# Storing output chunks as sixteen runs of rows, and loading the value block in 64 + 8 partitions

## The chip, the cores and the metric

The kernel runs on one core of one Trainium2 chip. The metric is the device time of one execution in microseconds (us), the median of repeated runs; lower is better. A separate execution is recorded by the hardware profiler, and all views below are of that one.

## What is computed

Two operators in a row. First an attention whose keys and values are averaged over groups of eight tokens; then a mixture of experts with one chosen expert per token, in which the chosen expert's answer is weighted by its probability.

```python
# q, k, v: (8 batches, 8 heads, 576 tokens, 64), float32
k_p = k.reshape(B, H, 72, 8, D).mean(axis=3)          # 72 groups of 8 tokens
v_p = v.reshape(B, H, 72, 8, D).mean(axis=3)
attn = softmax(q @ k_p.T / sqrt(D))
x = (attn @ v_p), heads side by side                  # (4608 tokens, 512)
logits = unit(x) @ unit(expert_emb).T / tau           # 8 experts
e = argmax(logits);  gate = softmax(logits)[e]
out = gate * (relu(x @ w1[e]) @ w2[e])                # w1 512x1024, w2 1024x512
```

The output is 4608 rows of 512 float32, 576 rows per batch.

## The kernel before, in words

**One batch after the other, 576 tokens each.** With T = 36, a token of a batch is `i * 36 + t`: i is one of 16 runs of 36 consecutive tokens, t the place in the run. `flat` (L295) puts (head, run) on the 128 partitions for q and k. `grouped` (L298) puts the 72 groups on partitions for v, so the value tile `vv` has 72 partitions. Loads are issued by GpSimd, which casts float32 to fp16 on the way.

**The steps of a batch** are made in `attention` (from L386) and `ffn` (from L732):

- `load_v` (L889) loads v in one transfer. For batch 0 `mean_raw` (L602) and `v_sum` (L455), both on TensorE, make the mean and the group sums from it; for later batches VectorE adds (L445, L449). From the mean of v, `guess` (L615) and `guess_end` choose one expert for the whole batch. GpSimd reads that choice into a register and issues the loads of the expert's w1 and w2 (`load_w1` L319, `load_w2` L324), or skips them where one of four held pairs of weights is that expert's already.
- The 36 places in a run are cut in three units of 12, u = 0, 1, 2: `score` (L471), `exp` (L478), `pv` (L489), `x_scale` (L499, L501), and `x_turn` (L507), a VectorE transpose in blocks of 32 that brings 192 tokens of x into `xt_all`, features on partitions. Columns of `xt_all` are ordered by place and then by run (`t * 16 + i`).
- `square` (L516) and `route` (L530) give the router's logits; `route_out`, `root` (GpSimd), `prob` and `gate` make the gate per token.
- `h_part` (L749) is the first layer: eight slices `w` of 128 hidden features, four matmuls of each block of tokens. The first two slices (`early` = 2) are done in three blocks of 192 tokens, so that they can start once the first unit is turned; the others in two blocks of 288. `relu` (L758) moves the sums to `hT`.
- `y_part` (L769) is the second layer, by chunks of 128 tokens (c = 0 to 3), and `y_last` (L798) the last 64 tokens. `y_out` (L786, L788) scales by the gate, and `store` (L877) writes the chunk to the output, through SyncE's queue, in the last batch through ScalarE's queue too.

**What a store looks like.** A chunk's 128 partitions are 8 places times 16 runs, place first. `out_rows` (L864) describes the destination in that order: 8 places outermost, 16 runs inside, rows of 2 KB. The last 64 tokens are two stores of 4 places by 16 runs by 1 KB.

**What orders the work.** Every step is entered in a `Plan` with an engine, a cost, what it waits for, a priority, PSUM tiles (`NPS` = 4) and, for loads and stores, a cost on the DMA rings. `order` places steps greedily, `improve` tries 400 random changes of the priorities and keeps what lowers the planned end of TensorE's work over six random draws. The steps are then emitted in that order on each engine; each engine works through its own list strictly. So a changed cost or dependence can change the order of the whole kernel. Where the plan has TensorE idle, `warm` (L371) emits filler matmuls on a tile of ones: one for 0.22 us of planned idle time, with slower ones reckoned in the first 5.5 us; from planned time 28 on only where over 0.4 us are idle, and for 65% of that.

**The end.** A loop (L1068) handles batches in which some token chose another expert than the batch's guess. It has as many rounds as a number made on the chip, and in this data none. On entering it, every engine waits for the transfers still in flight. After the loop the last full chunk, kept in `y_end`, is stored in two halves of 64 partitions, one from SyncE (L1113) and one from ScalarE (L1114).

Of the kernel before, what the change touches and what calls it, by code (L numbers as in the profile page):

```python
# [242 lines left out]
def kernel(  # L243
# [54 lines left out]
    def grouped(a, b):  # L298
        return a[b].rearrange("h (g r) d -> g h (r d)", r=POOL)
# [56 lines left out]
    def cols(c):  # L356
        return ds(c * 128, min(128, S - c * 128))


    def warm(slot, idle, t):  # L360

# [24 lines left out]
    def attention(b, early=False):  # L386
# [117 lines left out]

        def x_turn(u):

            nc.vector.transpose(  # L507
                out=xt_all[:, b].rearrange("p w (t l) -> p t w l", l=32)[:, ts(u, 6)],
                in_=st['x', u].rearrange("p b j d -> p (b j d)").rearrange(
                    "p (t l w) -> p t w l", w=4, l=32))  # L510

        def square(u):
            if 'sq' not in st:
                st['sq'] = xp.tile([128, 4, S], BF16, name="sq", bufs=1)
            cs = ts(u, 192)
            nc.scalar.activation(out=st['sq'][:, :, cs], in_=xt_all[:, b, :, cs],  # L516
                                 func=AF.Square)

# [185 lines left out]
        for u in range(NU):  # L704
            step(f's{u}', 'PE', 0.53, lambda u=u: score(u),
                 ['kT', f'q{u}', (f'pv{u}', b - 1)], b - 10, tiles=2)
            for p in range(2):
                step(f'e{u}{p}', 'ACT', 0.71, lambda u=u, p=p: exp(u, p), [f's{u}'], b - 5,
                     frees=[(f's{u}', p)])
            step(f'pv{u}', 'PE', 0.55, lambda u=u: pv(u), ['v', f'e{u}0', f'e{u}1'],  # L710
                 b - 10, tiles=1)
            step(f'xs{u}', 'DVE', 1.18, lambda u=u: x_scale(u), [f'pv{u}'], b - 1.5,
                 frees=[(f'pv{u}', 0)])
            step(f'x{u}', 'DVE', 0.92, lambda u=u: x_turn(u), [f'xs{u}'], b - 1.6)
            step(f'sq{u}', 'ACT', 0.75, lambda u=u: square(u),
                 [f'x{u}', ('route', b - 1)], b - 4)

        step('route', 'PE', 0.86, route,
             ['sq0', 'sq1', 'sq2', 'emb', ('h', 0, b), ('gate', b - 2)], b - 0.02, tiles=1)
# [12 lines left out]
    def ffn(plan, b, xt, w, get_gm, finish, last=False, early=0):  # L732
# [9 lines left out]
        def h_part(w, u):  # L742


            n, step_ = (SU, 256) if w < early else (HALF, 512)
            if u == 0:
                st['ph', w] = psum(plan)
            for kk in range(4):
                nc.tensor.matmul(out=st['ph', w][:, ds(u * step_, n)],  # L749
                                 lhsT=w1v[:, kk, w // 4, (w // 2) % 2, w % 2, :],  # L750
                                 rhs=xt()[:, kk, ts(u, n)],
                                 start=(kk == 0), stop=(kk == 3))

        def relu(w):
            n, step_ = (SU, 256) if w < early else (HALF, 512)
            if ('hT', w // 4) not in st:
                st['hT', w // 4] = hp_.tile([128, 2, 2, S], FP16, name=f"hT{w // 4}")
            nc.scalar.activation(  # L758
                out=st['hT', w // 4][:, (w // 2) % 2, w % 2, :].rearrange(
                    "p (r c) -> p r c", c=n),  # L760
                in_=st['ph', w].rearrange("p (r c) -> p r c", c=step_)[:, 0:S // n, 0:n],
                func=AF.Relu)

        def y_part(c, part):
            if part == 0 and (last or c % 2 == 0):
# [57 lines left out]
        for w, u in order:  # L823
            end = 2 if w < early else 1
            xs = before('lw1' if w < 4 else 'lw1b', 'copy',
                        *(f'x{i}' for i in range(u + 1 if w < early else u + 2)))
            hs[w, u] = chain(0.33 if w < early else 0.495, lambda w=w, u=u: h_part(w, u), xs,
                             tiles=int(u == 0))
# [12 lines left out]
        for part in parts:  # L841
            if part is None:
                o = chain(0.98, y_last, before('lw2', 'copy') + relus, 1)
                plan.step('ACT', 1.4 if last else 0.85, y_last_out, [o, *gm], -10 + pri,
                          frees=[(o, 0)], store=0.45)
                continue
            c, half = part
            ys[c, half] = chain(0.865, lambda c=c, half=half: y_part(c, half),
                                before('lw2', 'copy') + relus[4 * half:4 * half + 4],
                                tiles=int(half == 0 and (last or c % 2 == 0)))  # L850
            if half:
                o = ys[c if last else c // 2 * 2, 0]
                if last:
                    plan.step('DVE' if c % 2 == 0 else 'ACT', 0.7 if c % 2 == 0 else 1.2,
                              lambda c=c: y_out(c), [ys[c, 1], *gm], -10 + pri,
                              frees=[(o, 0)], store=0.82)
                elif c % 2:
                    for i in (c - 1, c):
                        plan.step('ACT', 0.6, lambda i=i: y_out(i), [ys[i, 1], *gm],
                                  -10 + pri, frees=[(o, 0)] if i == c else [], store=0.82)  # L860
        if b is not None:
            done['y', b] = prev[0][0]

    def out_rows(o_b, c, y_sb):  # L864

        rows = o_b.rearrange("(i t) d -> t i d", t=T)
        if c < 4:
            return [(rows[ts(c, 8)], y_sb)]
        DH = DM // 2
        return [(rows[32:T, :, ts(j, DH)], y_sb[ts(j, 64), 0:DH]) for j in range(2)]  # L870

    def store(b):
        o_b = out[ts(b, S)]
# [8 lines left out]
    with tc.manual_schedule():  # L882
# [6 lines left out]
        def load_v(b, after=()):  # L889
            def emit():  # L890
                vv = loads['v', b] = inp.tile([G, H, POOL * D], FP16, name="vv")
                nc.gpsimd.dma_start(out=vv, in_=grouped(v, b))
            done['lv', b] = load(0.9, 3.6, emit, [('v', b - 2), ('vs', b - 2), *after])

        def load_q(b, units=(NU,), u=0):
            def emit(cs):
# [213 lines left out]
            px.run()  # L1110

    for dst, src in out_rows(out[ts(B - 1, S)], 3, y_end):
        nc.sync.dma_start(out=dst[0:4], in_=src[0:64])  # L1113
        nc.scalar.dma_start(out=dst[4:8], in_=src[64:128])  # L1114

# [1 line left out]
_INS = ['q', 'k', 'v', 'moe_expert_emb', 'moe_tau', 'moe_w1', 'moe_w2']  # L1117
# [31 lines left out]
```

The softmax here doesn't subtract the row's maximum and nothing guards it: scores larger than these inputs give would overflow.

## Time and profile before

| | |
|---|---|
| time, median of 3 runs | 216.98 us (216.51 to 219.39) |
| the profiled execution | 220.48 us, span 218.8 us |
| mean granted TensorE clock | 0.941 |
| busy: TensorE / VectorE / ScalarE / GpSimd | 194.6 / 143.9 / 126.3 / 35.3 us |
| loads through GpSimd's queue | 24.65 MB, 61.8% of 16 DMA engines' span |
| stores through SyncE's queue | 9.00 MB, 12.8% of 16 DMA engines' span |

The span runs from the first to the last instruction of the profiled execution. A busy time is a sum over the span; it does not tell whether a stage waited. The granted clock is the share of full speed that TensorE was given; it is either 1 or 0.5 at a moment here. The share of a DMA queue is the time that its packets took, over 16 engines and the whole span.

### The profile page before, as it was taken

To read this page: it belongs to the slowest core of one execution; us is meant where nothing else is said; L and a number is where in the kernel's file an instruction comes from. 1 tells how busy PE (TensorE), PEld (TensorE's weight loads), DVE (VectorE), ACT (ScalarE), POOL (GpSimd) and SP (SyncE) were. 2 spreads that over 40 slices of the span, in tenths; PEclk is the share of its full clock that TensorE was granted. 3 is DMA by queue.
4 is the path that set the end of the run, shared out by engine and by line. 5 is a ranking of instruction groups with operands and counts; after the bars stand their busy time and mean duration, and the time that the engine had idled before them with its cause. 6 is when DMAs were issued, how large, how long until landed. Compare 5 with 4: busy or idle time off the path is not lost. (4 is left out here: it accounts for less than half of the span.)

```text
span 218.8 us, 7393 instructions
## 1 busy us (share of the span) xinstructions
PE 194.6 (89%) x3155; PEld 121.6 (56%) x3156; DVE 143.9 (66%) x391; ACT 126.3 (58%) x203; POOL 35.3 (16%) x61
## 2 busy tenths in 40 slices
PE   6869999998996999998898899989998999999910
PEld 2345477454873468555674487538753865486500
DVE  3644948559598943976699669775977894732200
ACT  3034526386476367557674967586758767775200
POOL 7107016000410007003010511041000020020000
PEclk9985589998898799999999999999999999999995
DMA  5997999999997148999994799999975500330131
GB/s 81 180 161 116 206 216 181 202 216 229 252 216 133 27 108 195 202 219 190 235 219 86 164 186 235 226 208 230 234 180 128 186 32 3 99 115 9 45 130 52
DMA packets 18486, 34.63 MB, mean 158 GB/s; under 512 B 2440, under 2 KB 9224, under 8 KB 17936
## 3 DMA queue, kind: packets, MB, share of 16 engines
q0 software_dynamic: 12992, 24.65, 61.8%
q1 hardware_dynamic: 5184, 9.00, 12.8%
q8 instruction: 26, 0.43, 0.8%
q10 hardware_dynamic: 272, 0.46, 0.6%
q14 instruction: 12, 0.10, 0.1%
HBM read 61.88 MB, written 9.44 MB: 326 GB/s over the span
## 5 line engine op out<-in xcount | busy, mean ns | idle before, releaser
L749 PE MATMUL pa<-xt_all,w 128*128 128x288 f16 (+1 forms) x576 | 68.7, 276 | 1.1 <-DVEq L666 0.6
L769 PE MATMUL pa<-w,hT 128*128 128x512 f16 x256 | 62.7, 386 | 4.0 <-ACT y_sb L786 2.8
L749 PEld LDWEIGHTS <-w 128*128 128x128 f16 x576 | 53.2, 99 | 14.5 <-issue 3.8
L758 ACT ACTIVATE hT<-pa 128x576 f16<-128x576 f32 x64 | 40.7, 647 | 19.2 <-PE pa L749 18.5
L478 ACT ACTIVATE at<-pa 72x768 f16<-72x768 f32 x48 | 36.6, 803 | 12.5 <-PE pa L471 12.1
L769 PEld LDWEIGHTS <-hT 128*128 128x128 f16 x256 | 23.4, 98 | 30.4 <-issue 6.6
L786 ACT ACTIVATE y_sb<-pa,gm 128x512 f32<-128x512 f32 x29 | 19.1, 685 | 25.0 <-PE pa L769 25.0
L516 ACT ACTIVATE sq<-xt_all 128x768 bf16<-128x768 f16 x24 | 20.0, 841 | 10.4 <-DVE xt_all L507 10.2
L432 DVE STREAM_TRANSPOSE qT<-qq 128x768 f16<-128x768 f16 x24 | 22.6, 961 | 3.9 <-DMA qq<-in_q_dram 3.6
L501 DVE TENSOR_TENSOR x_sb<-pa,rc 128x768 f16<-128x768 f32 x24 | 23.0, 957 | 0.8
L507 DVE STREAM_TRANSPOSE xt_all<-x_sb 128x768 f16<-128x768 f16 x24 | 22.9, 965 | 0.3
L371 PE MATMUL pa<-ones_m 128*128 128x512 f16 x58 | 18.7, 470 | 1.7 <-DVE half_c L975 1.7
L319 POOL DMA_DIRECT2D w<-in_moe_w_dram x10 | 4.2, 417 | 97.5 <-DMA w<-in_moe_w_dram 40.6
L499 DVE RECIPROCAL rc<-pa 128x12 f32<-128x12 f32 x24 | 5.3, 222 | 21.1 <-PE pa L489 20.6
L547 POOL TENSOR_TENSOR rn<-lgT,half_c 128x5 f32<-128x5 f32 x8 | 9.5, 1189 | 58.8 <-DVE lgT L552 58.8
L471 PE MATMUL pa<-qT,kT 32*72 32x192 f16 x384 | 14.6, 257 | 3.2 <-DVE kT L423 1.8
L489 PEld LDWEIGHTS <-at 72*32 72x32 f16 x1152 | 12.1, 101 | 8.9 <-ACT at L478 4.6
L489 PE MATMUL pa<-vpx,at 72*32 72x65 f16 x1152 | 15.0, 203 | 1.9 <-ACT at L478 1.4
L471 PEld LDWEIGHTS <-kT 32*72 32x72 f16 x384 | 8.6, 111 | 11.8 <-issue 5.6
L552 DVE STREAM_TRANSPOSE lgT<-pa 128x160 f32<-128x160 f32 x8 | 2.8, 349 | 16.4 <-PE pa L530 16.4
L445 DVE TENSOR_TENSOR vv<-vv 72x2048 f16<-72x2048 f16 (+1 forms) x14 | 13.1, 935 | 0.2
L371 PEld LDWEIGHTS <-ones_m 128*128 128x128 f16 x58 | 6.2, 115 | 9.0 <-issue 4.7
(98 smaller groups left out, 152.6 us busy)
## 6 DMA issues: line engine op xcount, KB each, us to landing
w<-in_moe_w_dram POOLq DMA_DIRECT2D x14, 1024.0 KB, 16.1
out_dram<-y_sb SPq DMA_DIRECT2D x30, 256.0 KB
kk<-in_k_dram POOLq DMA_DIRECT2D x8, 576.0 KB, 16.9
vv<-in_v_dram POOLq DMA_DIRECT2D x8, 576.0 KB, 25.0
qq<-in_q_dram POOLq DMA_DIRECT2D x7, 576.0 KB, 16.5
w<-in_moe_w_dram POOLq DMA_DIRECT2D x4, 512.0 KB, 6.3
out_dram<-y_sb SPq DMA_DIRECT2D x15, 64.0 KB
qq<-in_q_dram POOLq DMA_DIRECT2D x1, 384.0 KB
```

The source lines that it names most:

```text
L371: nc.tensor.matmul(out=pa[:, 0:512], lhsT=ones_m[:, 0:128], rhs=ones_m[:, 0:512], start=True, stop=True)
L432: nc.vector.transpose(out=qT.rearrange("p w r (t i) -> p t w r i", i=16), in_=qq.rearrange("p t (w r i) -> p t w r i", w=2, r=2))
L471: nc.tensor.matmul(out=pS[a // 2][0:G, ds(a % 2 * 512 + r * SU, SU)], lhsT=kT[ts(a, 32), w, r, :], rhs=qT[ts(a, 32), w, r, :], start=(w == ...
L478: nc.scalar.activation(out=at.rearrange("g a r c -> g a (r c)"), func=AF.Exp, scale=escale, in_=st['pS', u][p][0:G].rearrange("g (a c) -> ...
L489: nc.tensor.matmul(out=px[ts(a, 32), c0:c0 + D + 1], lhsT=st['at', u, a // 2][:, a % 2, r, ts(j, 32)], rhs=st['vpx'][:, 2 * a + r, 0:D + 1 ...
L501: nc.vector.tensor_tensor(out=x_sb, in0=pxv[:, :, :, 0:D], in1=rc.unsqueeze(3).to_broadcast([128, 2, 6, D]), op=ALU.mult)
L507: nc.vector.transpose(out=xt_all[:, b].rearrange("p w (t l) -> p t w l", l=32)[:, ts(u, 6)], in_=st['x', u].rearrange("p b j d -> p (b j d ...
L516: nc.scalar.activation(out=st['sq'][:, :, cs], in_=xt_all[:, b, :, cs], func=AF.Square)
L749: nc.tensor.matmul(out=st['ph', w][:, ds(u * step_, n)], lhsT=w1v[:, kk, w // 4, (w // 2) % 2, w % 2, :], rhs=xt()[:, kk, ts(u, n)], start ...
L758: nc.scalar.activation(out=st['hT', w // 4][:, (w // 2) % 2, w % 2, :].rearrange("p (r c) -> p r c", c=n), in_=st['ph', w].rearrange("p (r ...
L769: nc.tensor.matmul(out=py, lhsT=st['hT', w // 4][:, (w // 2) % 2, w % 2, ts(c, 128)], rhs=w2[:, w // 2, w % 2, :], start=(w == 0), stop=(w ...
L786: nc.scalar.activation(out=y_sb, in_=py, func=AF.Copy, scale=g)
```

## The change

Three things are done to the transfers, and the layout in between is adapted to the first.

1. **Order of rows.** Within each chunk of 128 tokens, columns are now ordered by run and then by place (`i * 8 + t`). The destination of a store becomes 16 runs outermost, 8 places inside (4 places in the last chunk), and the final `y_end` is cut by columns rather than by partitions, again with 16 runs outermost. The purpose is that a store is dealt to sixteen DMA engines.
2. **Value loads** are two transfers, of partitions 0 to 63 and of 64 to 71, instead of one of 72.
3. **What has to follow.** `x_turn` becomes two transposes per unit (four and two of the blocks of 32 tokens), which write a chunk's columns in steps of 8 elements (4 in the last chunk). As chunk 1 is completed only by unit 1, the three early blocks of `square` and `h_part` are now 128, 256 and 192 tokens wide (`third`), `square` waits for all units up to its own, and the early `relu` reads one continuous range of PSUM. The planner's costs of these steps are changed too.

```diff
+    def third(u):
+        return slice((0, 128, 384)[u], (128, 384, S)[u])
...
         def x_turn(u):
-            nc.vector.transpose(
-                out=xt_all[:, b].rearrange("p w (t l) -> p t w l", l=32)[:, ts(u, 6)],
-                in_=st['x', u].rearrange("p b j d -> p (b j d)").rearrange(
-                    "p (t l w) -> p t w l", w=4, l=32))
+            src = st['x', u].rearrange("p b j d -> p (b j d)").rearrange(
+                "p (m s i w) -> p m w s i", w=4, s=2, i=16)
+            m = 0
+            for c, n in ((0, 4), (1, 2), (1, 2), (2, 4), (3, 4), (4, 2))[2 * u:2 * u + 2]:
+                m0 = 2 if (c, u) == (1, 1) else 0
+                nc.vector.transpose(
+                    out=xt_all[:, b, :, cols(c)].rearrange(
+                        "p w (i m s) -> p m w s i", i=16, s=2)[:, m0:m0 + n],
+                    in_=src[:, m:m + n])
+                m += n
...
-            cs = ts(u, 192)
+            cs = third(u)
...
-            step(f'x{u}', 'DVE', 0.92, lambda u=u: x_turn(u), [f'xs{u}'], b - 1.6)
-            step(f'sq{u}', 'ACT', 0.75, lambda u=u: square(u),
-                 [f'x{u}', ('route', b - 1)], b - 4)
+            step(f'x{u}', 'DVE', 0.98, lambda u=u: x_turn(u), [f'xs{u}'], b - 1.6)
+            step(f'sq{u}', 'ACT', (0.54, 0.96, 0.75)[u], lambda u=u: square(u),
+                 [*(f'x{i}' for i in range(u + 1)), ('route', b - 1)], b - 4)
...
         def h_part(w, u):
-            n, step_ = (SU, 256) if w < early else (HALF, 512)
+            cs = third(u) if w < early else slice(u * HALF, u * HALF + HALF)
+            to = cs.start + 128 if w < early else u * 512
...
-        rows = o_b.rearrange("(i t) d -> t i d", t=T)
+        rows = o_b.rearrange("(i t) d -> i t d", t=T)
         if c < 4:
-            return [(rows[ts(c, 8)], y_sb)]
+            return [(rows[:, ts(c, 8)], y_sb)]
         DH = DM // 2
-        return [(rows[32:T, :, ts(j, DH)], y_sb[ts(j, 64), 0:DH]) for j in range(2)]
+        return [(rows[:, 32:T, ts(j, DH)], y_sb[ts(j, 64), 0:DH]) for j in range(2)]
...
-                nc.gpsimd.dma_start(out=vv, in_=grouped(v, b))
-            done['lv', b] = load(0.9, 3.6, emit, [('v', b - 2), ('vs', b - 2), *after])
+                for gs in (slice(0, 64), slice(64, G)):
+                    nc.gpsimd.dma_start(out=vv[gs], in_=grouped(v, b)[gs])
+            done['lv', b] = load(1.4, 3.1, emit, [('v', b - 2), ('vs', b - 2), *after])
...
     for dst, src in out_rows(out[ts(B - 1, S)], 3, y_end):
-        nc.sync.dma_start(out=dst[0:4], in_=src[0:64])
-        nc.scalar.dma_start(out=dst[4:8], in_=src[64:128])
+        for eng, cs in ((nc.sync, slice(0, DM // 2)), (nc.scalar, slice(DM // 2, DM))):
+            eng.dma_start(out=dst[:, :, cs], in_=src[:, cs])
```

Left out are the changed costs of stores (0.82 to 0.72, 0.45 to 0.4) and of the early parts of `h_part`, and the new `relu`.

More of the change, by code (lines that the diff above doesn't have):

```diff
@@ L748, in h_part @@
             for kk in range(4):
-                nc.tensor.matmul(out=st['ph', w][:, ds(u * step_, n)],
+                nc.tensor.matmul(out=st['ph', w][:, ds(to, cs.stop - cs.start)],
                                  lhsT=w1v[:, kk, w // 4, (w // 2) % 2, w % 2, :],
-                                 rhs=xt()[:, kk, ts(u, n)],
+                                 rhs=xt()[:, kk, cs],
                                  start=(kk == 0), stop=(kk == 3))
         def relu(w):
-            n, step_ = (SU, 256) if w < early else (HALF, 512)
             if ('hT', w // 4) not in st:
                 st['hT', w // 4] = hp_.tile([128, 2, 2, S], FP16, name=f"hT{w // 4}")
+            hT = st['hT', w // 4][:, (w // 2) % 2, w % 2, :]
+            if w < early:
+                nc.scalar.activation(out=hT, in_=st['ph', w][:, 128:128 + S], func=AF.Relu)
+                return
             nc.scalar.activation(
[L759 to L762, printed above, removed]
+                out=hT.rearrange("p (r c) -> p r c", c=HALF), func=AF.Relu,
+                in_=st['ph', w].rearrange("p (r c) -> p r c", c=512)[:, :, 0:HALF])
         def y_part(c, part):
@@ L826, in ffn @@
                         *(f'x{i}' for i in range(u + 1 if w < early else u + 2)))
-            hs[w, u] = chain(0.33 if w < early else 0.495, lambda w=w, u=u: h_part(w, u), xs,
+            hs[w, u] = chain((0.24, 0.44, 0.33)[u] if w < early else 0.495, lambda w=w, u=u: h_part(w, u), xs,
                              tiles=int(u == 0))
@@ L844, in ffn @@
                 plan.step('ACT', 1.4 if last else 0.85, y_last_out, [o, *gm], -10 + pri,
-                          frees=[(o, 0)], store=0.45)
+                          frees=[(o, 0)], store=0.4)
                 continue
@@ L855, in ffn @@
                               lambda c=c: y_out(c), [ys[c, 1], *gm], -10 + pri,
-                              frees=[(o, 0)], store=0.82)
+                              frees=[(o, 0)], store=0.72)
                 elif c % 2:
@@ L859, in ffn @@
                         plan.step('ACT', 0.6, lambda i=i: y_out(i), [ys[i, 1], *gm],
-                                  -10 + pri, frees=[(o, 0)] if i == c else [], store=0.82)
+                                  -10 + pri, frees=[(o, 0)] if i == c else [], store=0.72)
         if b is not None:
```

## The prediction, made before the changed kernel was run

> **What bounds the kernel now.** I read the page's 40 slices first (5.47 us each), then busy time by stretch, TensorE's timeline, and the timeline of the end.
>
> ```profile
> PE   6869999998996999998898899989998999999910
> PEclk9985589998898799999999999999999999999995
> DMA  5997999999997148999994799999975500330131
> ```
>
> TensorE is busy nearly throughout; the DMA engines are full from the second slice to about the twelfth; TensorE's clock is halved in slices 4 and 5. The windows (length, then busy us of TensorE and the others, granted clock, DMA share, GB/s) split this by stage: start, half clock, batch 0 up to the first layer of batch 1, batch 1, batches 2 to 7, end.
>
> ```profile
> 0.00:15.30 15.30, 10.81 (x122) 5.30 (x124) 6.65 (x40) 3.69 (x7) 5.03 (x15) 1.00 0.87 144
> 15.30:28.95 13.65, 13.14 (x206) 7.04 (x204) 10.33 (x22) 6.08 (x8) 4.19 (x6) 0.50 0.94 163
> 28.95:54.84 25.89, 24.51 (x396) 15.04 (x395) 17.07 (x54) 15.24 (x25) 4.58 (x8) 0.96 1.07 209
> 54.84:80.20 25.36, 23.50 (x380) 14.80 (x380) 20.33 (x48) 14.16 (x24) 3.15 (x4) 0.90 0.71 149
> 80.20:208.50 128.30, 122.63 (x2061) 79.43 (x2059) 89.03 (x229) 86.70 (x140) 18.35 (x28) 1.00 0.72 157
> 208.50:218.76 10.26, 0.02 (x1) 0.00 (x0) 0.48 (x1) 0.47 (x1) 0.00 (x0) 0.73 0.25 85
> ```
>
> So 128 us of the span are TensorE's own work, where neither a store nor a load ends a wait. A transfer can matter in two places only. One is the start, where batch 0's v is waited for (first line); from there to the first layer stand fillers, L371, at half clock:
>
> ```profile
> 13.31 0.84 PE L602 MATMUL pa<-ones_m,vv 72*64 72x1 f16 x33 [0.79 <-DMA vv<-in_v_dram]
> ...
> 23.63 2.74 PE L371 MATMUL pa<-ones_m 128*128 128x512 f16 x6
> 26.43 1.44 PE L749 MATMUL pa<-xt_all,w 128*128 128x192 f16 x8
> 27.66 2.10 PE L371 MATMUL pa<-ones_m 128*128 128x512 f16 x6
> 29.60 1.15 PE L749 MATMUL pa<-xt_all,w 128*128 128x192 f16 x12
> ```
>
> The other is the end: 10.26 us with almost no computing.
>
> ```profile
> 206.26 0.63 ACTq L877 DMA_DIRECT2D out_dram<-y_sb  x1
> 206.83 0.75 DVE L788 TENSOR_SCALAR y_sb<-pa,gm 128x512 f32<-128x512 f32 x1 [1.84 <-PE pa L769]
> 208.56 0.48 DVE L780 TENSOR_SCALAR y_end<-pa,gm 128x256 f32<-128x256 f32 x1 [0.98 <-PE pa L769]
> 209.19 0.47 ACT L782 ACTIVATE y_end<-pa,gm 128x256 f32<-128x256 f32 x1 [2.96 <-DVEq L1068]
> 212.90 1.06 ACTq L1114 DMA_DIRECT2D out_dram<-y_end  x1
> 214.06 0.59 SPq L1113 DMA_DIRECT2D out_dram<-y_end  x1
> ```
>
> `y_end` is ready at 209.66, but its stores are issued at 212.90 and 214.06: the loop's entry (L1068) waits for all stores in flight. In the trace's packet records the one that holds it, SyncE's chunk 2 issued at 207.61, moves its 128 packets from 209.93 to 211.87, and the entry is passed at 212.56.
>
> **What the skill says.** "DMA: Bandwidth & Descriptors", section "Why a DMA increments its semaphore by 16 and not by 1": a transfer is dealt to the largest number of engines, up to 16, that divides the outermost dimension of both sides. For the old stores that is 8, and 4 for the two small ones and the halves of `y_end`; for 72 partitions it is 12, though the section has an exception for some GpSimd transfers. The trace agrees for stores: SyncE's queue has 312 semaphore writes of 4 bytes, which is 30 x 8 + 15 x 4 + 4 for `y_end` + 8 for the embeddings. For v it fits: from 14 to 17 us, when v's packets are all that is left, they start at 100 per us against 163 per us before. "TensorE: Matmul & The Clock Gate", Part 1: TensorE runs at half clock after an idle window of about 3.4 us and at full clock after a busy one. The trace agrees: half clock from 15.30 to 28.95 is four times 3.41 us, after the idle time around 10 to 13 us. "SBUF — State Buffer", Door 1: accesses that each fall in a new line of 16 bytes pay a penalty, and the new transposes write in steps of exactly 16 bytes. No row of before has such a write; the nearest (L423) reads its inputs in steps of 128 bytes and takes 382 ns for 128 elements against some 295 for 32, that is 0.9 ns an element, no penalty.
>
> **The change part by part.**
>
> *Final stores.* 64 packets of 2 KB on each queue over four engines: 16 per engine at 84 ns, 1.3 us, and both queues use the same engines: SyncE's first packet (215.80) comes with ScalarE's first semaphore write. The data run from 214.12 to 217.47, 3.35 us. After: 128 packets of 1 KB over 16 engines, 8 each at 46 ns (this size's duration in the chunk-4 stores), 0.37 us per queue, so SyncE no longer queues behind. Its path becomes issue 214.06, plus 1.19 to first packet (the shortest seen, 203.77 to 204.96), plus 0.4: done at 215.7 instead of 217.47, **1.8 us less**. If descriptors come slower than engines take them (the slowest 64 here took 1.9 us), only 0.6 is left.
>
> *Loop entry.* Chunk 2's 128 packets have 16 per engine, 1.34 us, and start only as the ScalarE store before them ends. On 16 engines both halve: 8 x 84 = 0.67 us. The last semaphore would come some 1.3 to 1.9 us sooner, but ScalarE's own walk through the semaphores ends at 211.04, so at most 1.5 are gained. The issue-to-first-packet times here (1.2 to 2.3 us) may not shrink: 0.6 at worst. I take **1.0**. End together: 2.8, say **2.6** since one delay may hide in the other; bounds 1.2 and 3.3.
>
> *Other stores* (batches 0 to 6): nothing waits for them but the reuse of seven buffers; no wait on a store stands in the list. Nothing.
>
> *Value load of batch 0.* Twelve engines: 48 packets each at 98 ns, 4.7 us. Sixteen and then eight: 32 + 8, 3.9 us. Landing, and so L602, 0.8 us sooner. GpSimd pays about 0.45 us more per batch for a second issue (128 descriptors take 0.54, 576 take 0.87, so a fixed part of 0.45). GpSimd is busy 16% and what stands behind it, batch 0's q, then waits for the ring anyway; nothing. Later v are landed long before use (median 25 us from issue); nothing.
>
> *Transposes.* 768 elements take 965 ns, 576 take 775 (L507, L414): 0.99 ns an element and 0.2 fixed. Two per unit, less 0.1 overlap: 1.07, so 0.1 more per unit, 24 x 0.1 = 2.4 us of VectorE, which is at 66%. Behind it wait `square` and the early `h_part`. Hidden by other batches' matmuls in the 128 us stretch, on the path in batches 0 and 1: 0.2. With the penalty at its worst, double time per element, 0.75 more a unit.
>
> *Early blocks.* 128 + 256 + 192 columns are as many as 3 x 192; ScalarE's squares likewise. Nothing.
>
> *The order, which the diff does not show.* The built program's instruction order differs on every engine. In batch 0 the new one puts v's sums for batch 1, `mean` and `guess` of batch 1 ahead of the first layer, turns unit 0 of x last, and puts 30 fillers in one block before the first layer, where there were 6 and 6. Following the old durations in the new order, that block starts at 23.4. VectorE: the second `pv` ends about 21.7; its scaling and turn (0.2 + 1.0 + 1.1) end at 24.0, batch 1's guess at 25.3, then two more units of 2.3, so x is complete at about 29.8. Fillers: if full clock comes at 28.95, 13 at 0.43 us and 17 at 0.22 end at 32.6; if a window sooner, 30.9. So the first layer begins 4.5 to 6 us later than 26.43, but then runs without a pause: 24 matmuls at 0.08, 48 at 0.12 and routing 0.9 end at 39.8 to 41.4, against 38.2. In return the waits behind the second layer shrink: before, batch 1's last `score` (47.33) was followed by 7.5 us to the first layer of batch 1 (54.84), half of it idle or filler; now four second-layer matmuls and `y_last` lie behind that `score`, and the path `exp` 1.5, `pv` 0.6, scaling 1.2, turn 1.1 gives 5.5 to 6. First layer of batch 1: 54.3 to 56. I take **+0.4**, bounds -0.6 and +1.4.
>
> *Batch 3.* Before, TensorE waited here for the last unit of x:
>
> ```profile
> 103.81 0.50 PE L749 MATMUL pa<-xt_all,w 128*128 128x192 f16 x4
> 104.15 1.46 PE L371 MATMUL pa<-ones_m 128*128 128x512 f16 x6
> 106.23 0.94 PE L749 MATMUL pa<-xt_all,w 128*128 128x192 f16 x9 [0.63 <-DVEq L666]
> ```
>
> 2.1 us of filler and wait. The new order has no filler after batch 1, and the last `pv` of batch 3 stands ahead of 20 second-layer matmuls. That gains up to 2.1; since other waits of 0.3 to 0.7 us, of which there are some 20, can fall either way, I take **-1.0**, bounds -2.4 and +1.0.
>
> Sum: -2.6 + 0.2 + 0.4 - 1.0 = **-3.0, so 214.0 us**.
>
> **The rivals.**
> - *Forecast* (0.55): the end gives 2.6, the middle little. 214.0, within 2%.
> - *Everything gives* (0.22): 3.3 at the end, 2.4 in batch 3, 0.6 at the start: 216.98 - 6.3 = 210.7. For: a new order without fillers. Against: a half-clock spell costs 1.7 us, and such spells come after any idle window.
> - *The start eats it* (0.15): the filler block keeps TensorE until 32.6 and what follows keeps the delay, +3 instead of +0.4, with 0.6 + 0.6 at the end and nothing in batch 3: 216.98 - 1.2 + 0.2 + 3 = 219.0, slower but within 2%. For: the first layer does start later. Against: behind it stood waiting that can absorb it.
> - *Strided writes are slow* (0.08): 24 turns of 0.75 more; two units per batch exposed, 12 us, less 3.0: 226.0. For: the skill's line rule. Against: reads in such steps cost nothing.
>
> Range: the first two cases and most of the third, 210.5 to 218.5. Faster by over 2% (below 212.6): the second case and a part of the first, 0.30; slower by over 2% (above 221.3): 0.08; within: 0.62.
>
> **What would show it.** The stretch after TensorE's last matmul: 7.0 to 9.0 us instead of 10.26. SyncE's queue with about 16 semaphore writes per store. L602's start near 12.5. Transposes L517 of about 0.70 and 0.45 us. The 30 fillers ending at 31 to 33, the first layer of batch 1 near 55. It would be wrong if the transposes take over 0.9 us for four blocks, if the stores of the end take as long on 16 engines, or if the clock falls in a new place.

## The result: 21% slower, and the profile after

The changed kernel takes 264.49 us (median of 4 runs, 262.58 to 265.31), the kernel before 217.43 us beside it (216.51 to 219.39): a ratio of 1.214 (95% interval 1.203 to 1.225). The forecast was 214.0 us; the time lies outside its range and beyond its slowest rival.

The page's first part and its 40 slices (now 6.58 us each) come first.

```profile
PE 210.5 (80%) x3163; PEld 128.7 (49%) x3164; DVE 200.7 (76%) x415; ACT 123.9 (47%) x203; POOL 39.0 (15%) x69
...
PE   7899869897696968982999659975999189689990
...
PEclk9955868979799799996899979997999869979997
DMA  5979999976910099999603999599702200006033
```

Before, VectorE was busy for 143.9 us; now it is for 200.7. TensorE has holes in every batch where before its row was nearly all 8s and 9s, and its clock falls again and again. Most of the rise of TensorE's busy time comes from that: with contiguous writes (experiment 1), where the granted clock is 0.95 instead of 0.89, the same 3163 matmuls take 195.3 us. The holes have no common state of the DMA row: it has a 9 at TensorE's 2 and a 2 at TensorE's 1.

Busy time by stretch, cut at the same events as before (start, half clock and fillers, batch 0, batch 1, batches 2 to 7, end), columns as in the prediction:

```profile
0.00:15.30 15.30, 12.42 (x123) 5.96 (x125) 7.58 (x45) 3.19 (x7) 5.94 (x17) 0.96 0.91 155
15.30:35.30 20.00, 16.27 (x225) 7.99 (x223) 17.00 (x30) 4.14 (x7) 7.78 (x12) 0.67 1.00 179
35.30:67.45 32.15, 27.19 (x386) 16.84 (x387) 24.27 (x48) 15.51 (x25) 4.33 (x8) 0.85 0.94 184
67.45:94.40 26.95, 24.37 (x378) 14.69 (x378) 24.70 (x49) 13.51 (x22) 4.00 (x6) 0.87 0.33 64
94.40:256.40 162.00, 130.28 (x2055) 83.21 (x2053) 126.69 (x247) 87.05 (x142) 16.95 (x27) 0.93 0.57 126
256.40:263.10 6.70, 0.00 (x0) 0.00 (x0) 0.47 (x1) 0.47 (x1) 0.00 (x0) 0.76 0.32 87
```

The last six batches took 128.3 us before, with TensorE busy for 122.6; now they take 162.0, with TensorE busy for 130.3 and VectorE for 126.7 (89.0 before). Neither engine is full all the time: each waits for the other in places. The end is shorter, 6.7 us instead of 10.26.

What VectorE does in the added time stands in its groups by shape (line, names, shapes, count, busy us, mean ns, idle before):

```profile
L517 DVE STREAM_TRANSPOSE xt_all<-x_sb 128x512 f16<-128x512 f16 x24 | 60.2, 2537 | 3.2 <-ACT sq L527 2.8
L517 DVE STREAM_TRANSPOSE xt_all<-x_sb 128x256 f16<-128x256 f16 x24 | 30.1, 1254 | 0.2
```

The prediction had 0.70 and 0.45 us for these two; they take 2.54 and 1.25. The second mean mixes two kinds: sixteen of the 24 write in steps of 8 elements and take 1.42 us, the eight of the last chunk write in steps of 4 and take 0.93. Together the line is busy for 81.5 us, against 22.9 us of the one transpose per unit before. And the list of waits shows who pays (engine and line, what it waited for, total us, times, longest):

```profile
ACT sq L527 <- DVE xt_all L517: 36.1, 8, 14.3
...
PE pa L761 <- DVE xt_all L517: 21.5, 7, 6.4
```

TensorE's first layer now waits 21.5 us for the turn of x, a wait that is not among its long ones before, and ScalarE waits 36.1 us for the same line. Before, ScalarE's wait for the turn was 10.2, as the row of `square` in the profile of before has it (behind the second bar: idle time before it, and what ended most of that):

```profile
L516 ACT ACTIVATE sq<-xt_all 128x768 bf16<-128x768 f16 x24 | 20.0, 841 | 10.4 <-DVE xt_all L507 10.2
```

TensorE's timeline at the start (start us, length, line, count, idle before and its releaser):

```profile
12.35 1.46 PE L613 MATMUL pa<-ones_m,vv 72*64 72x1 f16 x64 [1.13 <-DMA vv<-in_v_dram]
...
22.99 9.01 PE L375 MATMUL pa<-ones_m 128*128 128x512 f16 x30
35.34 5.16 PE L761 MATMUL pa<-xt_all,w 128*128 128x128 f16 x28 [3.34 <-DVE xt_all L517]
...
67.45 0.61 PE L761 MATMUL pa<-xt_all,w 128*128 128x128 f16 x8 [2.98 <-DVE xt_all L517]
```

The first matmul on v (L613, L602 before) starts at 12.35 instead of 13.31, and the fillers end at 32.0, both near what was predicted (how much of the first is due to the change is taken up below). Then the first layer waits 3.34 us for L517, and the one of batch 1 comes at 67.45 where about 55 was predicted.

And the timeline of the end:

```profile
256.38 0.48 DVE L793 TENSOR_SCALAR y_end<-pa,gm 128x256 f32<-128x256 f32 x1 [0.97 <-PE pa L782]
256.90 0.47 ACT L795 ACTIVATE y_end<-pa,gm 128x256 f32<-128x256 f32 x1 [3.29 <-DVE y_end L793]
259.11 0.57 ACTq L1128 DMA_DIRECT2D out_dram<-y_end  x1
259.70 0.56 SPq L1128 DMA_DIRECT2D out_dram<-y_end  x1
```

`y_end` is ready at 257.37 and its first store is issued at 259.11, 1.74 us later; before it was 3.24 (209.66 to 212.90). From that issue to the end of the span it is 3.99 us; before 5.90. So the transfers did what they were meant to do. SyncE's queue shows 744 semaphore writes of 4 bytes: 16 for each of its 46 stores and 8 for the embeddings, which agrees with the rule on engines quoted in the prediction.

### The profile page after: what moved, and what is told of

Read it like the earlier page. It is cut to its first block, busy times and chain, and to the rows that moved or that the text cites. A ratio compares the mean times of both kernels' runs of the same rounds, so it can differ in the third digit from the quotient of the medians.

```text
span 263.1 us, 7440 instructions
## 1 busy us (share of the span) xinstructions
PE 210.5 (80%) x3163; PEld 128.7 (49%) x3164; DVE 200.7 (76%) x415; ACT 123.9 (47%) x203; POOL 39.0 (15%) x69
## 5 line engine op out<-in xcount | busy, mean ns | idle before, releaser
L761 PE MATMUL pa<-xt_all,w 128*128 128x288 f16 (+3 forms) x576 | 78.0, 295 | 25.2 <-DVE xt_all L517 21.5
L517 DVE STREAM_TRANSPOSE xt_all<-x_sb 128x512 f16<-128x512 f16 (+1 forms) x48 | 81.5, 1895 | 3.5 <-ACT sq L527 2.8
L761 PEld LDWEIGHTS <-w 128*128 128x128 f16 x576 | 56.1, 106 | 41.8 <-issue 24.0
L782 PE MATMUL pa<-w,hT 128*128 128x512 f16 x256 | 65.6, 405 | 12.3 <-ACT y_sb L799 6.3
L782 PEld LDWEIGHTS <-hT 128*128 128x128 f16 x256 | 24.8, 102 | 42.8 <-issue 13.1
L527 ACT ACTIVATE sq<-xt_all 128x768 bf16<-128x768 f16 (+2 forms) x24 | 19.6, 838 | 54.2 <-DVE xt_all L517 36.1
L375 PE MATMUL pa<-ones_m 128*128 128x512 f16 x66 | 20.3, 474 | 1.7 <-DVE half_c L989 1.7
L771 ACT ACTIVATE hT<-pa 128x576 f16<-128x576 f32 x16 | 9.9, 649 | 10.2 <-PE pa L761 10.2
L475 PE MATMUL pa<-qT,kT 32*72 32x192 f16 x384 | 13.8, 257 | 0.3 <-ACT y_sb L799 0.3
L375 PEld LDWEIGHTS <-ones_m 128*128 128x128 f16 x66 | 7.4, 117 | 12.0 <-issue 6.7
```

The source lines that it names most:

```text
L375: nc.tensor.matmul(out=pa[:, 0:512], lhsT=ones_m[:, 0:128], rhs=ones_m[:, 0:512], start=True, stop=True)
L475: nc.tensor.matmul(out=pS[a // 2][0:G, ds(a % 2 * 512 + r * SU, SU)], lhsT=kT[ts(a, 32), w, r, :], rhs=qT[ts(a, 32), w, r, :], start=(w == ...
L517: nc.vector.transpose(out=xt_all[:, b, :, cols(c)].rearrange("p w (i m s) -> p m w s i", i=16, s=2)[:, m0:m0 + n], in_=src[:, m:m + n])
L761: nc.tensor.matmul(out=st['ph', w][:, ds(to, cs.stop - cs.start)], lhsT=w1v[:, kk, w // 4, (w // 2) % 2, w % 2, :], rhs=xt()[:, kk, cs], s ...
L782: nc.tensor.matmul(out=py, lhsT=st['hT', w // 4][:, (w // 2) % 2, w % 2, ts(c, 128)], rhs=w2[:, w // 2, w % 2, :], start=(w == 0), stop=(w ...
```

## The experiments

The runs come in three groups, each with its own runs of the kernel before (218.84 us in 1 to 4, 218.72 in 5 to 8, 218.34 in 9 to 11, and 217.43 beside the changed kernel). A difference in us between kernels of two groups is good to about 1.4 us; the ratios don't have that doubt.

My theory: the transposes write in steps of 16 bytes, that makes them some three times as long, and this alone is the loss; the other parts do about what was forecast. Rivals: the new order of the plan is at fault; the number of instructions or the form of the transposes, not their step, makes them long; the transfers cost something that the end's gain hides.

**1. The same kernel with contiguous writes.** The two transposes per unit, the order of all instructions, stores and loads are those of the changed kernel; only the place of a column within its chunk differs, so that rows of a chunk land in each other's places.

```diff
-                        "p w (i m s) -> p m w s i", i=16, s=2)[:, m0:m0 + n],
+                        "p w (m s i) -> p m w s i", i=16, s=2)[:, m0:m0 + n],
```

> The changed kernel with one edit: its two transposes per unit write their columns one after the other instead of in steps of 8 (4 in the last chunk). Everything else, the order of instructions included, is the changed kernel's; rows within a chunk therefore come out in another order than the reference's. Theory A (the stepped writes are the whole loss): transposes of 512 elements take about 0.70 us and of 256 about 0.45, VectorE's busy time falls from 200.7 to about 146, and the time is 211 to 217. Theory B (the new instruction order, with its filler block and the late unit 0, is a main part of the loss): the transposes get as fast, but the time stays above 230.

Measured: 213.33 us (212.48 to 214.76), a ratio to the kernel before (218.84 beside it) of 0.975 (0.970 to 0.980). Its transposes by shape:

```profile
L517 DVE STREAM_TRANSPOSE xt_all<-x_sb 128x512 f16<-128x512 f16 x24 | 16.5, 692 | 0.4
L517 DVE STREAM_TRANSPOSE xt_all<-x_sb 128x256 f16<-128x256 f16 x24 | 10.0, 415 | 0.2
```

This one access pattern is worth 51 us. The same 48 instructions take 692 and 415 ns (0.70 and 0.45 were predicted), and the time comes near the forecast of 214.0. Their line is busy for 24.6 us instead of 81.5: 56.9 us of VectorE, 2.4 us per unit, of which 51.2 (264.49 less 213.33), that is nine tenths, reached the time.

**2. The changed kernel in the old order.** Only what the plan is told, costs and dependences, is put back.

```diff
-            step(f'x{u}', 'DVE', 0.98, lambda u=u: x_turn(u), [f'xs{u}'], b - 1.6)
-            step(f'sq{u}', 'ACT', (0.54, 0.96, 0.75)[u], lambda u=u: square(u),
-                 [*(f'x{i}' for i in range(u + 1)), ('route', b - 1)], b - 4)
+            step(f'x{u}', 'DVE', 0.92, lambda u=u: x_turn(u), [f'xs{u}'], b - 1.6)
+            step(f'sq{u}', 'ACT', 0.75, lambda u=u: square(u),
+                 [f'x{u}', ('route', b - 1)], b - 4)
...
```

The costs of the early `h_part`, of the stores and of `load_v` are put back likewise.

> The changed kernel whose plan is given the costs and dependences of the kernel before, so that its steps stand in the old order; stepped writes, new stores and split value loads stay, and the result is complete. Theory A: the transposes take 2.5 and 1.3 us as in the changed kernel and the time is 250 to 280. Theory B: the time is below 235.

Measured: 276.59 us, ratio 1.266 (1.258 to 1.274), its transposes at 2523 and 1263 ns. The new order isn't the cause; with transposes this long it is the better one by 12 us.

**3. The stores alone.** The kernel before with the new order of destination rows and `y_end` cut by columns; transposes, order and loads of before. Rows of a chunk land in each other's places.

```diff
-        rows = o_b.rearrange("(i t) d -> t i d", t=T)
+        rows = o_b.rearrange("(i t) d -> i t d", t=T)
...
-            return [(rows[ts(c, 8)], y_sb)]
+            return [(rows[:, ts(c, 8)], y_sb)]
```

> The kernel before with the new destination order of all stores and with y_end cut by columns; columns of xt_all keep their old order, so rows within a chunk are written to each other's places. Order of instructions as before. If the end is worth what the prediction took: stretch after TensorE's last matmul 7.0 to 9.0 us instead of 10.26, time 213.5 to 215.5 where the kernel before has 217. If it is hidden: 10 us and no difference.

Measured: 214.25 us (213.39 to 214.49), ratio 0.981 (0.977 to 0.986). The end of this kernel:

```profile
205.04 0.48 DVE L780 TENSOR_SCALAR y_end<-pa,gm 128x256 f32<-128x256 f32 x1 [0.98 <-PE pa L769]
205.56 0.47 ACT L782 ACTIVATE y_end<-pa,gm 128x256 f32<-128x256 f32 x1 [3.29 <-DVE y_end L780]
207.77 0.57 ACTq L1114 DMA_DIRECT2D out_dram<-y_end  x1
```

From the start of VectorE's half of `y_end` to the end of the span (211.7) it is 6.66 us, against 10.24 before (218.8 less 208.56): the 3.6 us at the end belong to the stores. They are most of the 4.6 us between the medians.

**4. Four step sizes in one kernel.** The changed kernel with another place for the columns in six of its batches: steps of one element (2 bytes) in batches 0 and 1, of two in 2 and 3, of four in 4 and 5 (there in pieces of 256 elements), and of eight, as the change has it, in 6 and 7. Rows land in each other's places in the first six.

```diff
+                    view = ("p w (m s i) -> p m w s i" if b < 2 else
+                            "p w (m i s) -> p m w s i" if b < 4 else
+                            "p w (i m s) -> p m w s i")
...
+                if b in (4, 5):
+                    for k in range(0, n, 2):
...
```

> The changed kernel, with the transposes of batches 0 and 1 writing next to each other, of 2 and 3 in steps of 2 elements (4 bytes), of 4 and 5 in steps of 4 (8 bytes, two blocks each), of 6 and 7 in steps of 8 (16 bytes) as in the changed kernel; rows of the first six batches come out in other orders. Theory L (the time goes by visits to lines of 16 bytes, about 4 ns each, beside 1 ns an element): per element 1 ns at steps 1 and 2, 2 ns at step 4, 4 ns at step 8, so 512 elements take about 0.7, 0.7, (twice 256: 0.5 to 0.9 each), 2.5 us. Theory C (any step costs, growing from the first): step 2 already takes over 1.2 us for 512 elements.

Measured: 228.43 us, a single run; only the durations are used. The transposes by shape, in three stretches of the span, one after the other (to 60 us batches 0 and 1, 60 to 110 batches 2 and 3, 110 to 165 batches 4 and 5 and the start of 6):

```profile
L527 DVE STREAM_TRANSPOSE xt_all<-x_sb 128x512 f16<-128x512 f16 x6 | 4.2, 698 | 0.1
L527 DVE STREAM_TRANSPOSE xt_all<-x_sb 128x256 f16<-128x256 f16 x6 | 2.5, 417 | 0.1
...
L527 DVE STREAM_TRANSPOSE xt_all<-x_sb 128x512 f16<-128x512 f16 x6 | 4.3, 726 | 0.5 <-ACT sq L537 0.5
L527 DVE STREAM_TRANSPOSE xt_all<-x_sb 128x256 f16<-128x256 f16 x6 | 2.6, 428 | 0.0
...
L519 DVE STREAM_TRANSPOSE xt_all<-x_sb 128x256 f16<-128x256 f16 x18 | 11.2, 760 | 0.5 <-ACT sq L537 0.3
L527 DVE STREAM_TRANSPOSE xt_all<-x_sb 128x512 f16<-128x512 f16 x2 | 5.1, 2561 | 0.0
L527 DVE STREAM_TRANSPOSE xt_all<-x_sb 128x256 f16<-128x256 f16 x2 | 2.8, 1412 | 0.0
```

For 256 elements, a step of 2 bytes takes 417 ns, 4 bytes 428, 8 bytes 760 and 16 bytes 1412. Neighbouring transposes overlap a little in these records, so the whole turn of a unit of 768 elements, from the first start to the last end, is the cleaner measure: 1.04, 1.06, 1.90 (in three pieces) and 3.61 us (the two units of a batch without the last chunk, whose own step is 8 bytes). So it isn't the stepping as such: 4 bytes are free, and from there the time about doubles with the step. The difference of the two shapes at 16 bytes, 2561 less 1412 over 256 elements, is 4.5 ns an element; at 2 bytes it is 1.1. That fits a cost per visited line of 16 bytes, worked out from these durations at about 4 ns each: one element in a line costs 4 ns, two cost 2 each, four cost 1 each, and that is the pace of the contiguous transposes. That the line is 16 bytes long is not shown by these runs: no step over 16 bytes was tried, so that the cost stops growing there was not seen. In all these forms, the fast ones too, the transposes read `x_sb` in steps of 8 bytes, so the penalty is one of the write. The Trainium skill, "SBUF — State Buffer", Door 1, names the line and the penalty, and the trace agrees that there is one. Where it says that two hits in a line are enough for full bandwidth, and that 8 elements of 2 bytes can be stepped for free, these writes differ: two hits (8 bytes) took 760 ns instead of 417, and a step of 8 elements is the slow case itself.

**5. The plan told the truth.** The changed kernel with one number altered, the plan's cost of a turn.

```diff
-            step(f'x{u}', 'DVE', 0.98, lambda u=u: x_turn(u), [f'xs{u}'], b - 1.6)
+            step(f'x{u}', 'DVE', 3.3, lambda u=u: x_turn(u), [f'xs{u}'], b - 1.6)
```

> The changed kernel with one number of the plan altered: a turn of x is entered at 3.3 us, about what it takes, where the change enters 0.98; the transposes themselves still write in steps of 16 bytes and should keep their 2.5 and 1.3 us. Theory A1, the order is at fault as much as the duration (the plan puts TensorE's early blocks and the routing behind turns that it believes short): with the true cost it hides much of the 58 us of VectorE, 225 to 245 us. Theory A2, the chain of a batch (scores, exp, sums, scaling, three turns, squares, routing) simply became some 8 us longer and nothing is there to fill it: 255 to 270, no better than the 264.5 of the changed kernel.

Measured: 242.75 us (241.76 to 243.56), ratio 1.110 (1.102 to 1.117); theory A1. The line and its two waits:

```profile
L517 DVE STREAM_TRANSPOSE xt_all<-x_sb 128x512 f16<-128x512 f16 (+1 forms) x48 | 81.6, 1893 | 2.7 <-PE pa L761 1.5 <-ACT sq L527 0.5
...
ACT sq L527 <- DVE xt_all L517: 23.4, 7, 5.7
PE pa L761 <- DVE xt_all L517: 3.9, 5, 1.2
```

VectorE does the same 81.6 us of turning, yet 21.7 of the 51 us are gone, and TensorE waits for a turn 3.9 us instead of 21.5. So some 40% of the loss goes with an order made for turns of 0.98 us; some 29 us stay under the order that knows. What those 29 are made of was not taken apart further.

**6. v in two transfers, alone.** The kernel before with the value loads of the change; plan and order of before.

```diff
-                nc.gpsimd.dma_start(out=vv, in_=grouped(v, b))
+                for gs in (slice(0, 64), slice(64, G)):
+                    nc.gpsimd.dma_start(out=vv[gs], in_=grouped(v, b)[gs])
```

> The kernel before with only the value loads in two transfers of 64 and 8 partitions; plan and instruction order of before. Forecast's step: the first matmul on v (L602, at 13.31 us before) starts 0.6 to 1.0 us sooner, but what it leads to waits for the clock and for fillers, and GpSimd's second issue is hidden: 217.5 to 219 beside some 218.5 of before, a ratio of 0.995 to 1.003. Rival, the start passes it on: 0.8 us or more off, ratio below 0.996. Rival, the second issue delays what stands behind it on GpSimd's ring (batch 0's q and the weights): ratio above 1.003.

Measured: 223.43 us (221.54 to 224.31), ratio 1.024 (1.017 to 1.031): slower, by the last theory of the three, though not at the place it named. GpSimd's timeline near batch 3:

```profile
79.70 1.33 POOL L893 DMA_DIRECT2D vv<-in_v_dram  x2
...
97.96 0.62 POOL L886 DMA_DIRECT2D kk<-in_k_dram  x1 [0.59 <-DVE x_sb L501]
101.01 0.54 POOL L900 DMA_DIRECT2D qq<-in_q_dram  x1 [2.43 <-DMA kk<-in_k_dram]
103.93 0.71 POOL L893 DMA_DIRECT2D vv<-in_v_dram  x1 [2.38 <-DMA qq<-in_q_dram]
109.05 0.60 POOL L893 DMA_DIRECT2D vv<-in_v_dram  x1 [4.41 <-DMA vv<-in_v_dram]
109.66 1.20 POOL L547 TENSOR_TENSOR rn<-lgT,half_c 128x5 f32<-128x5 f32 x1
```

The same place in the kernel before:

```profile
101.74 0.62 POOL L886 DMA_DIRECT2D kk<-in_k_dram  x1 [0.59 <-DVE x_sb L501]
102.35 0.55 POOL L899 DMA_DIRECT2D qq<-in_q_dram  x1
102.87 0.87 POOL L892 DMA_DIRECT2D vv<-in_v_dram  x1
108.86 1.20 POOL L547 TENSOR_TENSOR rn<-lgT,half_c 128x5 f32<-128x5 f32 x1 [5.12 <-DVE lgT L552]
```

In the built program GpSimd's transfers signal eight semaphores in turn, and an issue first waits for the transfer that last used its semaphore, eight issues before. The second half of v at 109.05 waits for the first half of the batch before, issued at 79.70 and landed at 108.76, and in both kernels `rn` of the routing stands behind v on GpSimd. Before, `rn` waited for its input `lgT` alone (ready at 108.78, `rn` at 108.86). With v in two, `lgT` is ready at 104.77 and `rn` starts at 109.66, 4.9 us late. TensorE, which was 4 us ahead of the kernel before at 104 us, then idles:

```profile
104.42 0.35 DVE L552 STREAM_TRANSPOSE lgT<-pa 128x160 f32<-128x160 f32 x1 [1.34 <-PE pa L530]
...
112.47 0.53 PE L471 MATMUL pa<-qT,kT 32*72 32x192 f16 x16 [3.08 <-ACT hT L758]
```

The columns `qT` for these scores stand behind `rn`'s successors on VectorE. The granted clock is 0.83 between 110 and 120 us, where the kernel before has 1.00.

**7. Only the last chunk by columns.** The kernel before with `y_end` stored by column halves over all 128 partitions, place outermost, so 8 engines for each half instead of 4.

```diff
-        nc.sync.dma_start(out=dst[0:4], in_=src[0:64])
-        nc.scalar.dma_start(out=dst[4:8], in_=src[64:128])
+        for eng, cs in ((nc.sync, slice(0, DM // 2)), (nc.scalar, slice(DM // 2, DM))):
+            eng.dma_start(out=dst[:, :, cs], in_=src[:, cs])
```

> The kernel before with one edit: the last chunk is stored by column halves over all 128 partitions (8 runs as outermost, so 8 engines for each half) and not by partition halves (4 engines each). Order of rows, transposes and all other stores are those of before. The loop's entry still waits for the stores in flight as before, so of the 3.6 us that the end lost in the changed kernel only the last burst's share should come: the stretch after the last matmul 8.5 to 9.5 us instead of 10.26, ratio 0.992 to 0.996. Rival, the whole gain came from the last stores: 6.7 to 7.5 us in that stretch, ratio 0.983 to 0.988. Rival, descriptors set the pace, not engines: 10.2, ratio 0.998 to 1.002.

Measured: 216.45 us (215.67 to 217.78), ratio 0.992 (0.989 to 0.996).

```profile
205.00 0.48 DVE L780 TENSOR_SCALAR y_end<-pa,gm 128x256 f32<-128x256 f32 x1 [0.98 <-PE pa L769]
205.52 0.47 ACT L782 ACTIVATE y_end<-pa,gm 128x256 f32<-128x256 f32 x1 [2.86 <-DVE y_end L780]
209.66 1.12 ACTq L1114 DMA_DIRECT2D out_dram<-y_end  x1
```

From `y_end` ready (205.99) to the first store it is 3.67 us, no less than the 3.24 before; from there to the end of the span (214.6) 4.94 instead of 5.90. So the last burst on 8 engines gives 1.0 of the 1.9 that 16 give, and the loop's entry gives nothing as long as chunk 2 goes on 8. The whole end, from VectorE's half of `y_end` on, is 9.6 us instead of 10.24. That is 0.6 of the 2.3 us between the medians (the interval allows 0.9 to 2.5); where the rest comes from is not shown.

**8. Both of these edits:** the last chunk by columns and v in two everywhere.

> The kernel before with both of these edits, the last chunk by column halves and v in two transfers; everything that writes contiguously before still does. If both only add up, a ratio of 0.990 to 0.996, that is the better of the two complete kernels without stepped writes; if the start passes the sooner v on, 0.985 to 0.991.

Measured: 221.00 us, ratio 1.012 (1.006 to 1.018). Both expectations were missed: the two edits do add up, but with the sign that experiment 6 gives the second.

**9. The last chunk by columns, and v in two in batch 0 alone.** After batch 0 every issue stands eight behind the same one as in the kernel before.

```diff
-                for gs in (slice(0, 64), slice(64, G)):
+                for gs in (slice(0, 64), slice(64, G)) if b == 0 else (slice(0, G),):
```

> The kernel before with the last chunk stored by column halves, and v in two transfers in batch 0 only; its result is complete. Theory Q: GpSimd's issues share eight semaphores in turn, so that each waits until the eighth before it has landed; v in two everywhere puts one more issue into each batch, and near 104 us its last one held GpSimd for 4.4 us and the routing's rn behind it. With one extra issue in batch 0 alone the later distances are those of before: no wait of vv on vv, rn on time, the first layer of batch 1 some 1 to 3 us sooner as in the run with v in two, and 212 to 215 us, a ratio of 0.970 to 0.988. Theory R, the loss with v in two lies in the transfers themselves (small ones of 8 partitions): batch 0's split brings nothing either, ratio 0.990 to 0.998, as the last chunk's edit alone.

Measured: 215.60 us (215.07 to 218.86), ratio 0.986 (0.981 to 0.992). Near batch 3:

```profile
100.43 0.87 POOL L893 DMA_DIRECT2D vv<-in_v_dram  x1 [0.93 <-DMA kk<-in_k_dram]
105.22 1.19 POOL L547 TENSOR_TENSOR rn<-lgT,half_c 128x5 f32<-128x5 f32 x1 [3.92 <-DVE lgT L552]
```

No wait of v on v, and `rn` waits for its input again: the loss of experiments 6 and 8 is gone, as theory Q has it, and the ratio is in its range, though 215.60 is a little above its 212 to 215 us. The edit takes away the small transfers of batches 1 to 7 along with their issues, so by itself it doesn't rule out that those transfers cost the time; what speaks for the waits is `rn` in experiment 6, and that the same transfers cost nothing in the new order (experiment 1 against 10). Whether batch 0's split brings something beyond experiment 7 stays open, since the two intervals overlap and in the profiled execution the first layer began no sooner (26.87, against 25.07 in experiment 7). Of the kernels here whose rows come out in place it has the best time: 1.4% faster than the one before, where the changed one is 21% slower.

**10 and 11. v in one, and v in two in batch 0 only, in the new order.** As experiment 1 (rows in each other's places) in all else.

> The changed kernel with the transposes writing contiguously (rows of a chunk land in each other's places) and v in one transfer everywhere; order of work, stores and the rest as in the changed kernel. Theory Q, with the loss of the old order (ratio 1.024 for v in two): 208 to 212 us, against 213.3 with v in two. Theory R2, the new order has room for the waits of v's second issue: 212.5 to 215.

> As the run before it, but v in two transfers in batch 0 alone. Theory Q: the first matmul on v about 0.8 us sooner and no wait of vv on an earlier transfer after batch 0: 207 to 211, at or up to 1.5 us under the run with v in one. Theory R2: 212.5 to 215, the same as with v in two everywhere.

Measured: 214.88 us (ratio 0.982, 0.976 to 0.989) and 214.09 us (0.981, 0.974 to 0.987), against 213.33 (0.975, 0.970 to 0.980) with v in two everywhere. Theory R2: in the new order v in two costs nothing that can be measured. The profile of experiment 1 shows why. VectorE and GpSimd near batch 3:

```profile
107.00 0.35 DVE L563 STREAM_TRANSPOSE lgT<-pa 128x160 f32<-128x160 f32 x1 [0.71 <-PE pa L541]
...
107.03 0.60 POOL L906 DMA_DIRECT2D vv<-in_v_dram  x1 [3.28 <-DMA vv<-in_v_dram]
107.64 1.23 POOL L558 TENSOR_TENSOR rn<-lgT,half_c 128x5 f32<-128x5 f32 x1
```

The issue waits 3.28 us there too, but `lgT` is ready only at 107.35, so `rn` is held up by 0.3 us.

## Why the prediction was wrong, step by step

- **Transposes: the step that failed.** The prediction named the line rule and the exact step of 16 bytes, and then priced it at "double time per element, 0.75 more a unit" in the worst case and at nothing in the forecast. Measured, the factor is four and the addition 2.4 us a unit (56.9 us over 24), three times the worst case. The prediction's own sign of being wrong, over 0.9 us for four blocks, is there: 2.54. The evidence used against the penalty was L423, which *reads* in steps of 128 bytes and loses nothing; the change *writes* in steps. A row with a stepped read can't price a stepped write. With no row of before showing such a write, the bound from above had to be open, and it was set at a factor of two with nothing measured behind it. The count of two transposes per unit was right: with contiguous writes the line takes 24.6 us, 1.02 a unit, against 1.07.
- **How much of it is exposed.** The rival took two units of three per batch; 51.2 us over 2.4 are 21 of 24. Part of that is the plan's wrong number for a turn: with the true one 29 us of the 51 remain (experiment 5). With the measured size and the rival's own share the sum would have been 217.0 + 16 x 2.4 - 3.0, some 252 us, still 12 short of the time.
- **Rivals.** "Strided writes are slow" was the right mechanism at 226.0; only its size and share were off. Its chance of 0.08 followed from the same misread L423.
- **Final stores and loop entry.** Right in direction and near in size: 1.9 us from the first issue to the end (1.8 predicted) and 1.5 from `y_end` to the first issue (1.0 predicted). The 1.8 is partly luck. It was to come from SyncE's store alone, with its issue where it was. In the packet records, the time from that issue to its last packet's end fell from 3.42 us (214.06 to 217.48) to 2.00 (259.70 to 261.70), that is 1.4; the other 0.6 came because SyncE's issue follows ScalarE's after 0.59 us instead of 1.16, which the prediction had held fixed. The reserve of 0.2 for delays that hide in each other wasn't needed. The stretch after the last matmul is 6.7 us, under the 7.0 to 9.0 named.
- **Value load of batch 0.** L613 starts 0.96 us sooner than in the profile of before, 0.8 predicted, but one pair of profiles can't show that. Over all profiles here the first matmul on v starts at 12.43 to 13.31 with v in one (the kernel before and experiments 3, 7 and 10) and at 11.91 to 12.84 with v in two: some 0.5 us between the means, and the two ranges overlap. "Later v ... nothing" and "GpSimd ... nothing" held in the new order only. In the old order the second issue costs 2.4% (experiment 6), through a wait on an older transfer that the prediction didn't look for: `rn` is queued behind v on GpSimd. Here two parts of the change hide each other.
- **Order and start.** The fillers end at 32.0 (31 to 33 predicted). Without the slow writes, batch 1's first layer starts at 60.34 and not near 55; the chain behind batch 0 was taken too short by 5 us. It comes back later: the first block of 288 columns in batch 3 starts at 106.89, against 108.31 before. Single pieces of the middle were wrong. Experiment 1 is 5.5 us under the kernel before, 3.5 of it at the end, which leaves about 2 for the middle where 0.4 was predicted. It isn't shown that the new order gives these 2: experiments 3 and 7, which leave the middle as it was, also gain 1.0 and 1.7 us beyond their ends.
- **Sum.** Without the failed step the time is 213.33 us, near the forecast of 214.0, but that is partly luck. The forecast took 3.0 off 216.98 us, a ratio of 0.986; experiment 1 takes 5.5 off the 218.84 measured beside it, and its interval of 0.970 to 0.980 leaves 0.986 out. Taken together, the other terms were right in sign and too small by some 2.5 us: 0.9 at the end, the rest as said above.

## What to carry to other kernels

Before a layout is moved into an operation's output, work out the step of its writes: for these VectorE transposes of 2-byte elements a step of 4 bytes was free, one of 8 took about double and one of 16 nearly four times as long, and an observation on reads said nothing about it. An upper bound that nothing measured supports is no bound; with 48 such instructions per kernel on a path that matters, one should be measured first. And where one engine's queue holds both transfers and computing, count its issues: here one more per batch moved a wait onto the computing behind it.

## What the runs showed that I had not expected

- A VectorE transpose of 128 x 256 fp16 takes 417, 428, 760 and 1412 ns with write steps of 2, 4, 8 and 16 bytes.
- Nine tenths of 56.9 us added to an engine that was 66% busy reached the time, though it was only 76% busy afterwards; telling the plan the true duration took back 21.7 us with the same busy time.
- A transfer's issue on GpSimd waited 4.4 us for a transfer eight issues older, issued 29 us before (experiment 6).
- Nearly half of the gain at the end hangs on a store that isn't the last one: 1.5 of 3.4 us come from the loop's entry, which waits for the stores in flight, chunk 2 among them.
